# One store per tile, wv in row halves, and a new order of steps in an attention and channel-mix kernel

## Chip, cores and metric

The kernel runs on one core of one Trainium2 chip. The metric is the device time of one execution in microseconds (us), as the median over several runs.

## What is computed

An attention with 32 memory slots per head feeds a channel-mix block. Eight batches, eight heads, 576 tokens of 64 values per head; the heads side by side make 512 columns, and the channel mix widens these to 1024.

```python
# q, k, v: (8, 8, 576, 64), phi: (8, 8, 576, 32)
a = softmax(phi, axis=tokens)
k_m = einsum('bhsm,bhsd->bhmd', a, k);  v_m = einsum('bhsm,bhsd->bhmd', a, v)
attn = softmax(q @ k_m.T / sqrt(64), axis=slots)
x = heads_side_by_side(attn @ v_m)               # (8, 576, 512)
x_prev = x shifted by one token (zero at the first)
xk = mu_k * x + (1 - mu_k) * x_prev              # the same for xr with mu_r
k = relu(xk @ w_k)                               # w_k: 512 x 1024
out = sigmoid(xr @ w_r) * (k * k @ w_v)          # w_r: 512 x 512, w_v: 1024 x 512
```

## The kernel before

All arithmetic on the matrix engine is in bf16; the loads from HBM convert from f32 on the way and are issued by GpSimd (`nc.gpsimd.dma_start`), since they cast. The first batch's phi is loaded from ScalarE's queue, and the two short vectors mu_k and mu_r, as four rows of 128 values each, from SyncE's queue (L147, L148).

The order of the work is written out by hand. `PLAN` is a list of words, and each word emits the instructions of one step; every engine works through its own instructions in the order in which they were emitted. The words are of these kinds:

- `p:k:1`, `p:wk:4-8` and the like issue a load: k, v, q or phi of a batch, or columns of a weight (in blocks of 128). `preload` is their function.
- `0:...` to `7:...` are steps of the attention of one batch: `exp` (exponential of phi on ScalarE), `k`, `v`, `ko`, `kov` (sums over the tokens, tile kvps, L279), `z`, `zk` (reciprocals), `nk`, `ak` (normalised k by VectorE or by ScalarE), `tk`, `ta` (its transposition), `q0`, `q1` (transposition of q on VectorE), `s`, `s0`, `s1` (scores and their exponential), `f..`, `q..` and `y..` (the sum over the slots, its reciprocal and the weighting, on VectorE), and for batch 0 `mk`, `mr` (the mixing with the previous token, tile mxps, L245) and `busy21x4` (21 idle matmuls of 4 blocks of 128 columns, L215, which fill time in which the matrix engine has nothing else).
- `x1:...` to `x8:...` build chunks of 512 tokens of x (`v`), the difference to the previous token (`d`) and the mixed inputs for keys and gates (`k`, `r`).
- `c0:5a`, `c1:3` and the like are keys: one block of 128 of the 1024 columns for one chunk of tokens (L617), the relu on ScalarE (L621) and the square on VectorE, or on ScalarE where the word ends in `s`.
- `g:5` is the gate of a tile of 128 tokens (L650, L653).
- `o:5` is the value and output of a tile: eight matmuls over the 1024 rows of wv (L667), one step on VectorE that multiplies by the gate into an f32 tile `o` (L669), and the store (L602). `o:1a` and `o:1b` are the left and the right half of the columns of tiles 0 to 3; the last tile, 35, is done in two halves too.

There are 36 tiles of 128 tokens. Tokens are held in an order in which a block of 64 neighbouring places stands for every ninth row of a batch, so a tile of 128 places is two blocks of 64 rows in HBM, and `store` issues one transfer for each block, from SyncE's queue; for the last two tiles the second block goes through ScalarE's queue. Four buffers hold `o`, four hold the gate `sg`, and `BANKS` gives the PSUM bank of every step that needs one. The squares `sq` are a ring of nine tiles, the mixed inputs a ring of four batches.

Of the kernel before, what the change touches and what calls it, by code (L numbers as in the profile page):

```python
# [10 lines left out]
F32 = mybir.dt.float32  # L11
# [5 lines left out]


PLAN = [
# [24 lines left out]
]  # L44

LOADS = {None: ("phi", "k", "v", "q")}
PRE = "k:0a id:"
BANKS = (
    "01234567012367540123675403612754036127546203715462073154620731546207315462037416520374165724031567240315"
    "67203415672034162053472053416720534720516372401637254016354106732541067325410673254173254173065412730652"  # L50
    "73041652730416527304165274163052741630527416305276413052764130527641305276413"
)


NJ = 9
# [6 lines left out]
def kernel(  # L62
# [13 lines left out]
    nc = tc.nc  # L76
    B, H, S, D = q.shape
    M = phi.shape[-1]
    Dm = H * D
    Dff = moe_w_k.shape[1]  # L80
    NTOK = B * S
    scale = 1.0 / (D ** 0.5)
    ND = Dm // 128
    NF = Dff // 128
    NPAIR = H // 2
    QR = S // NJ
# [10 lines left out]
    psum = ctx.enter_context(tc.psum_pool(name="psum", bufs=1))  # L97
# [4 lines left out]
    def bank():  # L102
        return f"ps{next(banks)}"
# [16 lines left out]
    def load_phi(b, eng):  # L120
        ph = ld.tile([128, HH, NJ, M], F32, name="ph", tag=f"ph{b % 2}")
        eng.dma_start(out=ph.rearrange("p h j m -> p h (j m)"), in_=rows(phi[b]))
        loads[b] = ph

    def load_rows(dst, src):
        nc.gpsimd.dma_start(out=dst.rearrange("p h j d -> p h (j d)"), in_=rows(src))
# [25 lines left out]
    wv_sb = big.tile([128, NF, Dm], BF16, name="wv")  # L152
# [7 lines left out]
    def preload(word):  # L160

        what, _, part = word.partition(":")
        if what in weights:
            dst, src = weights[what]
            f0, f1 = (int(x) * 128 for x in part.split("-"))
            nc.gpsimd.dma_start(out=dst[:, :, f0:f1], in_=src[:, :, f0:f1])
        elif what == "id":
            make_identity(nc, identity)
        else:
            n = int(part[0])  # L170
            if what == "phi":
                load_phi(n, nc.gpsimd)
            else:
                dst = qs[n % 2].rearrange("p (h j) d -> p h j d", j=NJ) if what == "q" else kvs[:, KV[n % 2]["k1v".index(what)]]
                src = {"q": q, "k": k, "v": v}[what][n]
                if len(part) == 1:
                    load_rows(dst, src)
                elif part[1] in "ab":
                    load_parity(dst, src, ROWS["ab".index(part[1])])
                else:  # L180
                    gs = slice(2 * int(part[1]), 2 * int(part[1]) + 2)
                    nc.gpsimd.dma_start(out=dst[:, gs].rearrange("p h j d -> p h (j d)"), in_=rows(src)[:, gs])
# [16 lines left out]
    for g in range(4):  # L199
        r = slice(g * M, (g + 1) * M)  # L200
# [8 lines left out]
    sq = big.tile([128, NF, 2 * S], BF16, name="sq")  # L209
# [379 lines left out]
        return steps  # L589


    def store(o, t, cols):
        g = t * 128
        eng = nc.sync
        while g < (t + 1) * 128:
            b, r = divmod(g, S)
            p = g - t * 128
            j, p0 = divmod(r, QR)
            j = (j + 1) % NJ if b else j
            n = min(QR - p0, (t + 1) * 128 - g)  # L600
            dst = out[b].rearrange("(p j) d -> p j d", j=NJ)[p0:p0 + n, j, cols]
            eng.dma_start(out=dst, in_=o[p:p + n, cols])  # L602
            if t >= NTOK // 128 - 2:
                eng = nc.scalar
            g += n

    def keys(c):
        start = STARTS[c]
# [28 lines left out]
    gated, outs, homes, parts = {}, {}, {}, {}  # L637
    free = {"sg": list(range(SG)), "o": list(range(4))}

    def take(name, t):  # L640
        homes[name, t] = free[name].pop(0)
        return work.tile([128, Dm], F32, name=name, tag=f"{name}{homes[name, t]}")
# [10 lines left out]
            nc.scalar.activation(gated[t], pr, AF.Tanh, scale=0.5)  # L653
        return go

    def value(t, hs=((0, 1),), n=1):

        def go():
            if t not in outs:
                outs[t] = take("o", t)  # L660
            o = outs[t]
            p = t * 128 % (2 * S)
            for h0, h1 in hs:
                cols = slice(h0 * Dm // n, h1 * Dm // n)
                pv = psum.tile([128, Dm], F32, name="pv", tag=bank())
                for fi in range(NF):
                    nc.tensor.matmul(pv[:, cols], lhsT=sq[:, fi, p:p + 128],  # L667
                                     rhs=wv_sb[:, fi, cols], start=(fi == 0), stop=(fi == NF - 1))
                nc.vector.scalar_tensor_tensor(o[:, cols], in0=gated[t][:, cols], scalar=1.0, in1=pv[:, cols],  # L669
                                               op0=AL.add, op1=AL.mult)  # L670
                store(o, t, cols)
                parts[t] = parts.get(t, 0) + Dm * (h1 - h0) // n
            if parts[t] == Dm:
                for name in free:
                    free[name].append(homes[name, t])
        return go

    NT = NTOK // 128
    chunks = {f"x{c}": chunk_steps(c) for c in range(1, len(STARTS))}
    mixes = {f"c{c}": keys(c) for c in range(len(STARTS))}  # L680
    mixes["g"] = {str(t): gate(t) for t in range(NT)}
    mixes["o"] = {str(t): value(t) if t < NT - 1 else value(t, ((0, 1), (1, 2)), 2) for t in range(NT)}
    for t in range(4):
        for h in range(2):
            mixes["o"][f"{t}{'ab'[h]}"] = value(t, ((h, h + 1),), 2)

    attend = [attention(b) for b in range(B)]
    todo = []
    for n, word in enumerate(" ".join(PLAN).split()):
        who, _, name = word.partition(":")  # L690
# [40 lines left out]
```

## Time and profile before

| | |
|---|---|
| median of 3 runs | 201.68 us (201.15 to 201.99) |
| profiled execution, its own time | 200.59 us |
| its span from first to last instruction | 198.8 us |
| mean granted TensorE clock | 0.991 |
| TensorE busy | 189.0 us (95%) |
| VectorE busy | 155.5 us (78%) |
| ScalarE busy | 149.7 us (75%) |
| GpSimd busy | 29.8 us (15%) |
| DMA issues of the output | 79 from SyncE, 3 from ScalarE |
| HBM read, written | 38.28 MB, 9.44 MB |

How to read the lines below. PE is TensorE's matmuls, PEld its weight loads, DVE is VectorE, ACT is ScalarE, POOL is GpSimd and SP is SyncE; an engine's name with a q behind it is its queue of instructions. In the rows of digits the span is cut into 40 equal slices, and each digit is the busy share of a slice in tenths. A DMA queue's line gives packets, megabytes, and the time that its packets took as a share of 16 DMA engines' span; the DMA share of a stage is over 1 where packets overlap on an engine. In groups of instructions "x80 | 9.2, 273 | 0.0" is the count, the busy time in us, the mean of one in ns, and the idle time just before them. In lines in order of time the first two numbers are the start and the length in us, and brackets hold the idle time before it and what ended it. A line on DMA issues gives the count, the size on the SBUF side and the median us from issue to landing.

### The profile page before, as it was taken

The page shows a single profiled execution, that of the slowest core. Times are in us where ns is not written, and L with a number is a line of the kernel's source. Part 1 is how long each engine was busy: PE and PEld are TensorE (multiplying, and loading weights), DVE is VectorE, ACT ScalarE, POOL GpSimd, SP SyncE. Part 2 cuts the span into 40 slices and gives each one's busy share as a digit, 9 for nine tenths or more (in the row PEclk, how much of TensorE's full clock was granted, in tenths as well). Part 3 has the DMA queues.
Part 4 walks back from the last instruction along what each step waited for, and adds up shares of the span by engine and source line. Part 5 has one row for each costly group of instructions (what it writes and reads, how often), then busy time and mean ns, then how long its engine had stood idle before and what let it go on. Part 6 is the DMA issues. An engine that isn't in the chain of part 4 may idle for free.

```text
span 198.8 us, 5486 instructions
## 1 busy us (share of the span) xinstructions
PE 189.0 (95%) x2194; PEld 97.4 (49%) x2214; DVE 155.5 (78%) x428; ACT 149.7 (75%) x307; POOL 29.8 (15%) x45
## 2 busy tenths in 40 slices
PE   8978799999999999999999999999999999999992
PEld 3535565784454544445347644444443445444451
DVE  6179589898879998999699999998999998122232
ACT  2245899748987999999998899997878698935210
POOL 7843323211050210003500000000000000000000
PEclk9979999999999999999999999999999999999999
DMA  6999999999999999994999903212142027004345
GB/s 160 183 206 268 206 208 199 267 224 276 250 224 279 232 302 218 266 299 64 207 208 248 227 2 83 53 31 53 44 108 63 1 47 167 0 3 106 81 97 139
DMA packets 24522, 31.30 MB, mean 157 GB/s; under 512 B 1960, under 2 KB 19632, under 8 KB 24496
## 3 DMA queue, kind: packets, MB, share of 16 engines
q0 software_dynamic: 17392, 20.91, 56.4%
q1 hardware_dynamic: 6336, 9.18, 17.9%
q10 hardware_dynamic: 768, 0.85, 1.4%
q8 instruction: 17, 0.28, 0.5%
q14 instruction: 9, 0.07, 0.1%
HBM read 38.28 MB, written 9.44 MB: 240 GB/s over the span
## 4 chain that ended last, share of the span: by engine, by line
PE 70%; DMA 13%; DVE 9%; ACT 3%; issue 1%; POOL 1%; POOLq 0%; DVEq 0%
PE pv L667 26%; PE pk L617 25%; PE pr L650 13%; DMA wr<-in_moe_w_r_dram 9%; DMA q<-in_q_dram 4%; PE kvps L279 3%; DVE o L669 1%; DVE diff L545 1%; DVE sq L629 1%; PE scps L371 1%; PE nops L245 1%; ACT x L536 1%; ACT sg L653 1%; DVE xrT L567 1%; DVE lz L422 1%
## 5 line engine op out<-in xcount | busy, mean ns | idle before, releaser
L617 PE MATMUL pk<-xkT,wk 128*128 128x512 bf16 (+4 forms) x344 | 67.3, 340 | 1.0 <-ACT xkT L458 0.3
L667 PE MATMUL pv<-wv,sq 128*128 128x512 bf16 (+1 forms) x324 | 65.3, 353 | 0.2
L621 ACT ACTIVATE rl<-pk 128x512 bf16<-128x512 f32 (+3 forms) x80 | 42.9, 555 | 6.8 <-PE pk L617 4.2
L617 PEld LDWEIGHTS <-wk 128*128 128x128 bf16 x352 | 32.9, 98 | 29.3 <-issue 1.5
L667 PEld LDWEIGHTS <-sq 128*128 128x128 bf16 x328 | 31.4, 98 | 29.5 <-issue 0.4
L650 PE MATMUL pr<-wr,xrT 128*128 128x512 bf16 x136 | 34.8, 380 | 0.6 <-DMA wr<-in_moe_w_r_dram 0.2
L669 DVE SCALAR_TENSOR_TENSOR o<-sg,pv 128x512 f32<-128x512 f32 (+1 forms) x41 | 24.4, 614 | 11.5 <-PE pv L667 11.4
L560 ACT ACTIVATE mu_d<-diff,mu 128x512 bf16<-128x512 bf16 (+1 forms) x40 | 26.2, 716 | 6.1 <-DVE diff L550 2.9
L653 ACT ACTIVATE sg<-pr 128x512 f32<-128x512 f32 x36 | 20.9, 601 | 9.4 <-PE pr L650 5.7
L629 DVE TENSOR_TENSOR sq<-rl 128x320 bf16<-128x320 bf16 (+5 forms) x63 | 17.6, 314 | 12.2 <-ACT rl L621 11.9
L627 ACT ACTIVATE sq<-rl 128x512 bf16<-128x512 bf16 (+5 forms) x41 | 21.7, 543 | 1.1
L650 PEld LDWEIGHTS <-xrT 128*128 128x128 bf16 x144 | 13.5, 98 | 16.5 <-issue 0.8
L536 ACT CAST x<-nops 128x512 bf16<-128x512 f32 (+3 forms) x34 | 16.0, 572 | 2.0 <-PE nops L245 2.0
L431 DVE TENSOR_TENSOR atn<-e,lz 128x320 bf16<-128x320 bf16 (+1 forms) x32 | 13.2, 442 | 0.2
L545 DVE TENSOR_TENSOR diff<-x 128x1024 bf16<-128x1024 bf16 (+1 forms) x15 | 10.5, 699 | 2.6 <-ACT x L536 2.6
L422 DVE STREAM_TRANSPOSE lz<-se 128x320 f32<-128x320 f32 (+3 forms) x22 | 12.3, 572 | 0.2
L376 ACT ACTIVATE e<-scps 128x288 bf16<-128x288 f32 x32 | 10.5, 421 | 2.4 <-PE scps L371 2.4
L265 ACT ACTIVATE em<-ph 128x1152 bf16<-128x1152 f32 (+1 forms) x9 | 9.3, 1053 | 3.5 <-DMA ph<-in_phi_dram 3.5
L356 DVE STREAM_TRANSPOSE qT<-q 128x576 uint32<-128x576 uint32 x16 | 11.9, 757 | 0.0
L215 PE MATMUL idle<-zeros 128*128 128x512 bf16 (+2 forms) x44 | 10.9, 414 | 1.0 <-DVE zeros L144 1.0
L413 DVE TENSOR_REDUCE se<-eT 128x18 f32<-128x576 bf16 (+3 forms) x16 | 11.1, 696 | 0.2
L279 PE MATMUL kvps<-kvs,em 64*32 64x64 bf16 (+2 forms) x864 | 10.0, 220 | 1.2 <-DMA kvs<-in_k_dram 1.2
(72 smaller groups left out, 148.1 us busy)
## 6 DMA issues: line engine op xcount, KB each, us to landing
out_dram<-o SPq DMA_DIRECT2D x61, 128.0 KB, 2.5
kvs<-in_v_dram POOLq DMA_DIRECT2D x8, 576.0 KB, 15.5
ph<-in_phi_dram POOLq DMA_DIRECT2D x7, 576.0 KB, 18.8
kvs<-in_k_dram POOLq DMA_DIRECT2D x7, 576.0 KB, 19.0
q<-in_q_dram POOLq DMA_DIRECT2D x6, 576.0 KB, 18.9
q<-in_q_dram POOLq DMA_DIRECT2D x4, 288.0 KB, 10.1
out_dram<-o SPq DMA_DIRECT2D x18, 64.0 KB, 5.6
wk<-in_moe_w_k_dram POOLq DMA_DIRECT2D x2, 512.0 KB, 14.3
```

Source lines behind the costliest of these rows:

```text
L279: nc.tensor.matmul(kvps[c][g * M:(g + 1) * M], lhsT=em[ROWS[c], j, g, :], rhs=kvs[ROWS[c], at, g, j, :], start=j == 0, stop=j == NJ - 1, s ...
L422: nc.vector.transpose(st["lz"].rearrange("p c (b t h) -> p (c b) h t", t=PB, h=2)[:, b0:b0 + n], st["se"][:, b0:b0 + n].unsqueeze(3).to_br ...
L536: (nc.vector.tensor_copy if both and i % 2 else nc.scalar.copy)(x[:, i, c0:c1], pss[i])
L560: nc.scalar.activation(t[:, i, :n], ds[c][:, pr + i, :n], AF.Copy, scale=mu1[:, o:o + 1])
L617: nc.tensor.matmul(pk[:, p0 - lo:p1 - lo], lhsT=wk_sb[:, di, fi * 128:(fi + 1) * 128], rhs=xk_T[:, di, p0 % RING:p0 % RING + p1 - p0], sta ...
L621: nc.scalar.activation(rl, pk, AF.Relu, scale=HALF_ROOT)
L627: nc.scalar.activation(sq[:, fi, p:p + p1 - p0], rl[:, part], AF.Square)
L629: nc.vector.tensor_mul(sq[:, fi, p:p + p1 - p0], rl[:, part], rl[:, part])
L650: nc.tensor.matmul(pr, lhsT=xr_T[:, di, c0:c0 + 128], rhs=wr_sb[:, di, :], start=(di == 0), stop=(di == ND - 1))
L653: nc.scalar.activation(gated[t], pr, AF.Tanh, scale=0.5)
L667: nc.tensor.matmul(pv[:, cols], lhsT=sq[:, fi, p:p + 128], rhs=wv_sb[:, fi, cols], start=(fi == 0), stop=(fi == NF - 1))
L669: nc.vector.scalar_tensor_tensor(o[:, cols], in0=gated[t][:, cols], scalar=1.0, in1=pv[:, cols], op0=AL.add, op1=AL.mult)
```

## The change

- The second half of wv's columns (2-4) is loaded in two transfers, rows of the lower and of the upper half of its eight row blocks (`wv:2-4l`, `wv:2-4u`). The first half of the columns is loaded as before.
- For tiles 0 to 3 the value of half the columns can be worked out in two steps, over row blocks 0 to 3 and 4 to 7 of wv, which add into the same PSUM bank (`o:3e` then `o:3f`, `o:3c` then `o:3d`). The new order uses that for four of the eight halves, and takes tiles 0 to 3 otherwise in half columns as before. `value` also gains halves for the last four tiles; the new order uses `34a` and `34b`, and does tile 35 whole.
- `store` issues one transfer for a tile where its second block goes to higher rows than its first, with an access pattern of two blocks, 64 rows and the columns; where it does not (tiles 8, 17, 26 and 35), two transfers, both from SyncE's queue.
- `PLAN` and `BANKS` are written anew: the loads of batch 1's phi and k now come ahead of wk, the first half of wv ahead of v of batch 1, more idle matmuls stand in batch 0, and the steps of all batches, chunks, keys, gates and outputs stand in another order, with other choices between VectorE and ScalarE.

```diff
 PLAN = [
-    "0:exp0 p:k:0b 0:busy3x3 0:busy21x4 0:mu 0:mub 0:exp1 0:k0c 0:k1c p:q:00 0:z 0:ha0 0:busy2x2 p:q:01 0:hn1 0:q0",
-    "0:q1 0:hc1 p:v:0 0:ht0 0:s1 0:fe1 0:fs1 0:s0 0:busy8x2 0:fo1 0:l1 0:l0 0:y2 0:v 0:nr0 0:h1z 0:busy4x2 p:wk:4-8",
-    "0:nr1 p:phi:1 0:h0z 0:y0 0:busy6x2 0:nk0 0:nk1 0:y1 0:y3 0:mk0 p:q:11 p:k:1 0:mk1 c0:5a 1:exp c0:4a c0:6as",
-    "c0:7bs 0:mr1 1:ko 1:zk0 1:zk1 p:wk:0-4 1:nk p:q:10 c0:4b 1:q1 c0:7a 1:ta 0:mr0 c0:0a 1:q0 c0:0b c0:3b c0:1a",
-    "c0:2a 1:s1 p:wr:0-4 p:v:1 1:s0 1:fe1 1:fs1 c0:2b c0:3as 1:qo2 1:qe1 g:2 1:qs1 g:0 p:wv:0-2 1:qo3 1:y2 g:3 1:qe0",
-    "g:1 1:qs0 1:qo0 1:y0 c0:1b 1:qo1 1:y3 1:y1 1:v 1:av c0:5bs c0:6b x1:v0m o:1a x1:v1 x1:d2d o:3a x1:d0d p:wv:2-4",
...
-    "c8:1 c8:0s x8:r2d c8:5s c7:3s c7:5 g:35 c7:2s g:30 c7:0s c7:7 g:29 o:29 o:30 g:28 g:32 c8:7 c8:6s o:28 g:31 o:32",
-    "g:33 o:33 g:34 o:31 o:34 o:35",
+    "p:q:00 0:exp1 p:k:0b 0:exp0 0:busy30x4 0:z 0:k1c p:q:01 0:k0c 0:ha1 0:hc1 0:q0 0:q1 0:hn0 0:mub 0:s1 0:qe2 0:hc0",
+    "0:qe3 0:busy3x3 0:fs1 0:busy6x2 0:fo1 0:s0 p:v:0 0:busy4x1 0:y2 0:busy2x1 0:v1c 0:l0 0:l1 0:nr1 p:phi:1 p:k:1",
+    "0:v0c 0:h0z 0:y3 0:h1z 0:y0 0:nr0 0:y1 0:busy9x3 0:nk0 1:exp 0:nk1 0:mr0 0:mr1 1:ko0c 0:mk1 1:ko1c p:wk:4-8",
+    "1:zk1 0:mk0 p:wk:0-4 1:zk0 0:mu 1:nk c0:4bs c0:5a c0:5b c0:6a p:q:10 1:ta 1:q0 c0:4as c0:7bs c0:3b c0:0a c0:2b",
+    "p:q:11 c0:2as 1:q1 c0:1a c0:6b c0:1b 1:s1 1:qe2 1:qe3 p:wr:0-4 1:fs1 1:s0 1:qe1 1:qo3 c0:7as c0:0bs p:wv:0-2",
+    "1:qs1 c0:3as 1:qe0 1:qo2 1:qs0 g:1 1:qo0 1:qo1 g:3 1:y2 1:y1 g:2 1:y0 p:v:1 g:0 o:3e 1:y3 o:2a o:0a 1:v 1:nv",
+    "o:3f x1:v1m p:wv:2-4l o:3c x1:v0m p:wv:2-4u x1:d2d o:1e p:phi:2 x1:d0d x1:k0d x1:k2e 2:exp o:0c o:0d o:2b o:1f",
...
+    "x8:k0e o:25 c7:7s g:29 c7:1 x8:r0d x8:r2e c7:2 c8:6 c7:4s c7:3 c7:0 c8:3 c8:2s c8:5 g:28 c8:0 c8:7s g:33 c8:4s",
+    "g:31 c8:1s o:31 g:30 o:33 g:34 o:29 g:35 o:30 o:34b g:32 o:35 o:32 o:28 o:34a",
 ]
...
-            nc.gpsimd.dma_start(out=dst[:, :, f0:f1], in_=src[:, :, f0:f1])
+            fis = {"l": slice(0, NF // 2), "u": slice(NF // 2, NF)}.get(part[-1], slice(0, None))
+            nc.gpsimd.dma_start(out=dst[:, fis, f0:f1], in_=src[:, fis, f0:f1])
...
     def store(o, t, cols):
-        g = t * 128
-        eng = nc.sync
-        while g < (t + 1) * 128:
+        at = []
+        for g in (t * 128, t * 128 + QR):
             b, r = divmod(g, S)
-            p = g - t * 128
-            j, p0 = divmod(r, QR)
-            j = (j + 1) % NJ if b else j
-            n = min(QR - p0, (t + 1) * 128 - g)
-            dst = out[b].rearrange("(p j) d -> p j d", j=NJ)[p0:p0 + n, j, cols]
-            eng.dma_start(out=dst, in_=o[p:p + n, cols])
-            if t >= NTOK // 128 - 2:
-                eng = nc.scalar
-            g += n
+            at.append(b * S + ((r // QR + 1) % NJ if b else r // QR))
+        if at[0] < at[1]:
+            dst = flat[at[0]:, cols]
+            ap = [[(at[1] - at[0]) * Dm, 2], [NJ * Dm, QR], [1, cols.stop - cols.start]]
+            nc.sync.dma_start(out=bass.AP(tensor=dst.tensor, offset=dst.offset, ap=ap), in_=o[:, cols])
+        else:
+            for n, row in enumerate(at):
+                nc.sync.dma_start(out=flat[row:row + (QR - 1) * NJ + 1:NJ, cols], in_=o[n * QR:(n + 1) * QR, cols])
...
-    def value(t, hs=((0, 1),), n=1):
+    def value(t, hs=((0, 1),), n=1, f0=0, f1=NF):
...
+                pv = opened.get(t) if f1 - f0 < NF else None
+                fresh = pv is None
+                if fresh:
+                    pv = psum.tile([128, Dm], F32, name="pv", tag=bank())
...
+                for fi in range(f0, f1):
+                    nc.tensor.matmul(pv[:, cols], lhsT=sq[:, fi, p:p + 128], rhs=wv_sb[:, fi, cols],
+                                     start=(fi == 0 and fresh), stop=(fi == NF - 1),
+                                     skip_group_check=f1 - f0 < NF)
+                if f1 < NF:
+                    continue
```

More of the change, by code (lines that the diff above doesn't have):

```diff
@@ L48 @@
 BANKS = (
-    "01234567012367540123675403612754036127546203715462073154620731546207315462037416520374165724031567240315"
-    "67203415672034162053472053416720534720516372401637254016354106732541067325410673254173254173065412730652"
-    "73041652730416527304165274163052741630527416305276413052764130527641305276413"
+    "01234567012436571026453106274531026753106753104267531042675310426753104275310427531027463150274631502746"
+    "31502746315072314560314572603145726031426013426013426570134260134265703126570431265704365704123675012436"
+    "0124753601247536012475360124753601245736015234756021437560214375602143756021"
 )
@@ L164, in preload @@
             dst, src = weights[what]
-            f0, f1 = (int(x) * 128 for x in part.split("-"))
-            nc.gpsimd.dma_start(out=dst[:, :, f0:f1], in_=src[:, :, f0:f1])
+            f0, f1 = (int(x) * 128 for x in part.rstrip("lu").split("-"))
+            fis = {"l": slice(0, NF // 2), "u": slice(NF // 2, NF)}.get(part[-1], slice(0, None))
+            nc.gpsimd.dma_start(out=dst[:, fis, f0:f1], in_=src[:, fis, f0:f1])
         elif what == "id":
@@ L589, in chunk_steps @@
         return steps
+    flat = out.rearrange("b s d -> (b s) d")
     def store(o, t, cols):
-        g = t * 128
-        eng = nc.sync
-        while g < (t + 1) * 128:
+        at = []
+        for g in (t * 128, t * 128 + QR):
             b, r = divmod(g, S)
-            p = g - t * 128
-            j, p0 = divmod(r, QR)
-            j = (j + 1) % NJ if b else j
-            n = min(QR - p0, (t + 1) * 128 - g)
-            dst = out[b].rearrange("(p j) d -> p j d", j=NJ)[p0:p0 + n, j, cols]
-            eng.dma_start(out=dst, in_=o[p:p + n, cols])
-            if t >= NTOK // 128 - 2:
-                eng = nc.scalar
-            g += n
+            at.append(b * S + ((r // QR + 1) % NJ if b else r // QR))
[6 more added lines that the diff above has]
+                nc.sync.dma_start(out=flat[row:row + (QR - 1) * NJ + 1:NJ, cols], in_=o[n * QR:(n + 1) * QR, cols])
     def keys(c):
@@ L654, in gate @@
         return go
-    def value(t, hs=((0, 1),), n=1):
+    opened = {}
+    def value(t, hs=((0, 1),), n=1, f0=0, f1=NF):
         def go():
-            if t not in outs:
-                outs[t] = take("o", t)
-            o = outs[t]
             p = t * 128 % (2 * S)
@@ L664, in go @@
                 cols = slice(h0 * Dm // n, h1 * Dm // n)
[L665 to L668, printed above, removed]
+                pv = opened.get(t) if f1 - f0 < NF else None
+                fresh = pv is None
+                if fresh:
+                    pv = psum.tile([128, Dm], F32, name="pv", tag=bank())
+                if f1 - f0 < NF:
+                    opened[t] = pv
+                for fi in range(f0, f1):
[4 more added lines that the diff above has]
+                    continue
+                if t not in outs:
+                    outs[t] = take("o", t)
+                o = outs[t]
                 nc.vector.scalar_tensor_tensor(o[:, cols], in0=gated[t][:, cols], scalar=1.0, in1=pv[:, cols],
@@ L672, in go @@
                 parts[t] = parts.get(t, 0) + Dm * (h1 - h0) // n
-            if parts[t] == Dm:
+            if parts.get(t) == Dm:
                 for name in free:
@@ L681 @@
     mixes["g"] = {str(t): gate(t) for t in range(NT)}
-    mixes["o"] = {str(t): value(t) if t < NT - 1 else value(t, ((0, 1), (1, 2)), 2) for t in range(NT)}
+    mixes["o"] = {str(t): value(t) for t in range(NT)}
+    for t in range(NT - 4, NT):
+        for name, h, n in (("a", (0, 1), 2), ("b", (1, 2), 2), ("i", (0, 3), 4), ("j", (3, 4), 4)):
+            mixes["o"][f"{t}{name}"] = value(t, (h,), n)
     for t in range(4):
@@ L685 @@
             mixes["o"][f"{t}{'ab'[h]}"] = value(t, ((h, h + 1),), 2)
+            mixes["o"][f"{t}{'ec'[h]}"] = value(t, ((h, h + 1),), 2, 0, NF // 2)
+            mixes["o"][f"{t}{'fd'[h]}"] = value(t, ((h, h + 1),), 2, NF // 2, NF)
+        mixes["o"][f"{t}l"] = value(t, f1=NF // 2)
+        mixes["o"][f"{t}u"] = value(t, f0=NF // 2)
     attend = [attention(b) for b in range(B)]
```

32 rows, old and new, of the table PLAN are left out of this document.

## The prediction

> **What bounds the kernel now.** I read the page first, then busy time by stage, then the DMA answers of short windows.
>
> ```profile
> PE 189.0 (95%) x2194; PEld 97.4 (49%) x2214; DVE 155.5 (78%) x428; ACT 149.7 (75%) x307; POOL 29.8 (15%) x45
> PE   8978799999999999999999999999999999999992
> DMA  6999999999999999994999903212142027004345
> q0 software_dynamic: 17392, 20.91, 56.4%
> q1 hardware_dynamic: 6336, 9.18, 17.9%
> ```
>
> TensorE is the bound: 189.0 of 198.8 us. The 9.8 us that it idles lie at the two ends of the second row. The third row shows a second limit behind it: the 16 DMA engines are full from the first slice to about 115 us and have room only after that. So there is little to gain on TensorE, and much to lose if a transfer is made slower.
>
> ```profile
> 10.00:15.00 5.00, 3.85 (x51) 1.89 (x48) 3.58 (x9) 2.05 (x6) 2.13 (x3) 0.73 1.22 207
> 15.00:20.00 5.00, 4.27 (x129) 2.78 (x129) 4.66 (x13) 2.73 (x9) 1.83 (x3) 0.93 1.17 267
> 20.00:25.00 5.00, 3.84 (x118) 2.71 (x123) 2.61 (x11) 4.29 (x11) 1.50 (x2) 1.00 1.23 207
> 25.00:30.00 5.00, 4.59 (x85) 2.97 (x80) 4.29 (x13) 4.55 (x14) 1.48 (x2) 1.00 1.23 207
> ...
> 5.00:38.00 33.00, 29.49 (x600) 18.09 (x600) 23.64 (x66) 22.35 (x58) 13.21 (x18) 0.95 1.24 219
> 38.00:97.00 59.00, 58.43 (x857) 30.09 (x863) 53.69 (x140) 51.44 (x106) 12.46 (x17) 1.00 1.09 237
> 97.00:115.00 18.00, 17.89 (x203) 11.00 (x198) 16.96 (x53) 16.33 (x31) 0.20 (x1) 1.00 1.11 217
> 115.00:198.80 83.80, 79.18 (x537) 36.67 (x542) 58.17 (x158) 58.10 (x114) 0.00 (x0) 1.00 0.28 64
> ```
>
> After the span follow TensorE's busy time, then the other engines', the granted clock, the DMA share and GB/s. TensorE idles 0.73 + 1.16 + 0.41 = 2.3 us between 15 and 30 us, 0.57 us from 38 to 97 and 0.11 us from 97 to 115; of the last stage's 4.6 us, 3.8 are the tail after the last matmul. The DMA share is 1.24, 1.09, 1.11, then 0.28.
>
> **The stores.** Before, a tile of 128 tokens leaves in two stores of 64 rows. After, where the two blocks go to rising rows, one store carries both, and its pattern on the HBM side begins with a dimension of size 2 (two blocks), then 64 rows. What sets how many engines a store runs on?
>
> ```profile
> DMA packets 173, 0.19 MB, mean 66 GB/s; under 512 B 4, under 2 KB 173, under 8 KB 173
> q1 hardware_dynamic: 8, 0.00, 0.3%
> mu<-in_moe_mu_k_dram SPq DMA_DIRECT2D x1, 2.0 KB
> ```
>
> ```profile
> DMA packets 160, 0.26 MB, mean 66 GB/s; under 512 B 32, under 2 KB 32, under 8 KB 160
> q1 hardware_dynamic: 160, 0.26, 28.8%
> ```
>
> ```profile
> GB/s 197 262 246 164 164 49 0 0 0 164 279 131 197 197 197 377 434 303 344 254 164 221 271 279 230 148 8 0 0 0 0 0 0 0 0 0 0 0 0 0
> ```
>
> These are the DMA answers for 0 to 2.9 us, 184 to 188 us and 194 to 199 us. In the first window SyncE's queue (q1) moved 8 packets, and 4 packets of all were under 512 bytes: the mu load of four rows of 512 bytes is four row packets and four small completion packets. In the second, one tile's two stores are 128 row packets and 32 small ones: 16 completions for each store of 64 rows. The page's 6336 is the same count: 79 × (64 + 16) + 2 × (4 + 4). So the engines on which a transfer runs follow the size of its outermost dimension: 4 for four rows, 16 for sixty-four. I read from this that an outermost size of 2 gives two engines. No run here shows a pattern of 2 on one side with 128 on the other, so this is an inference, and the main one. The Trainium skill ("DMA: Bandwidth & Descriptors", section "Why a DMA increments its semaphore by 16 and not by 1") says it outright: the engine count is the largest number up to 16 that divides the slowest dimension of both sides. By that rule it is two; the trace agrees for 4 and 16.
>
> Price on two engines. Of 36 tiles, four (8, 17, 26, 35) have falling rows and keep two stores; 32 are merged. The 9.18 + 0.26 MB of all stores are 0.262 MB a tile, so 8.39 MB are merged, 4.19 MB for each of two engines instead of 0.52. The best slice of the third fence moved 434 GB/s, 27.1 an engine: 4.19 MB take 155 us, 4.8 us a tile. From the other side, the second window's 28.8% of 4 us on 16 engines for 128 rows is 144 ns a row, and 64 rows one after another are 9.2 us a tile, 295 us in all. I take 155: that 144 ns is with 16 engines writing at once. The skill's page gives 27 GiB/s for an engine; by that figure it would be an estimated 145 us.
>
> The same two engines carry a sixteenth each of every load. 20.91 MB at the 219 GB/s of 5 to 38 us are 95.5 us, the same on each engine. The four unmerged tiles add 2.4 us (1.05 MB on 16 engines at 27.1). Sum on either engine: 95.5 + 155 + 2.4 = 253 us, more than the whole span now. A load has landed only when its slowest engine is done, so from the first store (about 38 us) on every load runs at the pace of those two. I allow 1.7 us ahead of the first load's packets (an estimate within the first window's 2.9), and the third fence's last packets lie 1.4 us before the end: 1.7 + 253 + 1.4 = 256 us of span. The profiled execution lasted 200.6 us for a span of 198.8, and lies 1.1 us under the median of 201.7: 256 + 1.8 + 1.1 = 259 us.
>
> What waits then: a store that has not landed holds one of four o buffers; the vector step at L669 (`scalar_tensor_tensor` into o) waits for the buffer, and behind it on VectorE stand the attention, squares and mixing of the next chunk, on which TensorE's keys wait.
>
> **What removing stores saves.** 79 + 3 issues become about 46, at about 0.63 us of queue time each (1.89 for three, below). SyncE's queue does nothing else, so that is worth nothing except at the end.
>
> ```profile
> 194.03 1.89 SPq L602 DMA_DIRECT2D out_dram<-o  x3
> 194.04 2.04 ACTq L602 DMA_DIRECT2D out_dram<-o  x3
> 195.01 0.42 DVE L669 SCALAR_TENSOR_TENSOR o<-sg,pv 128x256 f32<-128x256 f32 x1 [0.45 <-PE pv L667]
> ```
>
> Now the last half tile (35) leaves by two queues at once; after, half of tile 34 leaves in one store from SyncE, 0.66 us behind tile 28's (0.92 of matmul, 9.2 us for ten half tiles in the next fence, + 0.42 − 0.68 of vector time). On 16 engines I book 0 (−0.3 to +0.6); on two engines it is in the sum above.
>
> **wv in row halves and values in two steps.**
>
> ```profile
> L667 PE MATMUL pv<-wv,sq 128*128 128x256 bf16 x80 | 9.2, 273 | 0.0
> L669 DVE SCALAR_TENSOR_TENSOR o<-sg,pv 128x512 f32<-128x512 f32 x31 | 20.5, 678 | 10.9 <-PE pv L667 10.9
> ...
> L166 POOL DMA_DIRECT2D wv<-in_moe_w_v_dram x2: 873/878/884, 17.1 to 18.6; - x2
> L215 PE MATMUL idle<-zeros 128*128 128x512 bf16 x21 | 6.5, 479 | 0.0
> L215 PE MATMUL idle<-zeros 128*128 128x256 bf16 x20 | 3.5, 331 | 0.0
> L215 PE MATMUL idle<-zeros 128*128 128x384 bf16 x3 | 1.1, 516 | 1.0 <-DVE zeros L144 1.0
> ```
>
> Splitting a value into fi 0–3 and 4–7 leaves its eight matmuls as they are, so TensorE pays nothing; one bank stays taken between the steps, covered while seven others turn. One load more is 0.88 us of GpSimd, which is 15% busy: hidden. The idle matmuls grow from 133 to 174 blocks of 128 columns; 11.1 us for 133 make 41 more cost 3.4 us. They stand where TensorE waits for the first loads, which hides them; uncovered, they cost up to 3.4.
>
> **Order at the front.**
>
> ```profile
> 6.01 0.80 POOL L122 DMA_DIRECT2D ph<-in_phi_dram  x1
> 6.76 0.75 POOL L182 DMA_DIRECT2D q<-in_q_dram  x1
> 7.45 0.82 POOL L126 DMA_DIRECT2D kvs<-in_k_dram  x1
> ```
>
> ```profile
> ph<-in_phi_dram POOLq DMA_DIRECT2D x1, 576.0 KB, 12.3
> q<-in_q_dram POOLq DMA_DIRECT2D x1, 288.0 KB, 12.8
> ```
>
> ```profile
> kvs<-in_k_dram POOLq DMA_DIRECT2D x1, 576.0 KB, 15.5
> ```
>
> ```profile
> 17.50 1.36 PE L245 MATMUL mxps<-atn,vm 32*64 32x320 bf16 x40 [0.36 <-DVE vm L441]
> 19.12 2.32 PE L617 MATMUL pk<-xkT,wk 128*128 128x320 bf16 x16 [0.26 <-ACT xkT L458]
> 21.37 0.42 PE L245 MATMUL mxps<-atn,vm 32*64 32x256 bf16 x16
> 22.96 0.80 PE L279 MATMUL kvps<-kvs,em 64*32 64x128 bf16 x72 [1.16 <-DMA kvs<-in_k_dram]
> 24.88 0.48 PE L245 MATMUL mxps<-atn,vm 32*64 32x320 bf16 x24
> 29.97 3.63 PE L650 MATMUL pr<-wr,xrT 128*128 128x512 bf16 x15 [0.22 <-DMA wr<-in_moe_w_r_dram]
> ```
>
> GpSimd's queue hands loads over in order. Before, half of wk comes ahead of batch 1's phi and k, and k lands at 7.45 + 15.5 = 22.95. After, phi and k come first and the q half (1.3 us: 19.6 against phi's 18.3) moves behind wk, so the first half of wk lands near 22.95 − 1.3 = 21.6, and the first key, now at 19.12, starts 2.5 us later. TensorE has for that gap the mixing of r (0.42 + 0.48 us) and batch 1's k sums (0.80), 1.7 us; and the 1.16 us wait goes, since k lands early. Net 2.5 − 1.7 − 1.16 = −0.4 us. Up to wr the bytes are the same, so wr stays at 29.9, and the keys, three of whose halves now run behind the gates (L650), fill the time up to it. Behind 38 us TensorE idles under 1 us until 115, so no order gains more than that. It can cost: VectorE is busy 53.69 of 59 us and 16.96 of 18 there, so a vector step put late delays keys by its own length, 0.4 to 0.7 us; I book 0 and leave it to the second rival.
>
> **Rivals.** *First, the merged stores run on 16 engines* (the generator splits by the 128 rows on the SBUF side, or cuts the transfer in two, so that the change does not do what it says in the hardware). For it: each 64-row block alone ran on 16; against it: the count of 4 above. Then only the front is left: −0.4 and, where the order closes all of the 2.3 us, −2.3; in the middle 201.7 − 1.35 = 200.3 us, faster. It decides whether mixing r is done when wk lands at 21.6.
>
> *Second, the same without the luck*: batch 0's scores are split, its second half standing behind the mu matmuls and a copy on ScalarE, so the mixing starts late and the extra idle matmuls delay it in place of covering it. If mixing of k begins after about 20.2 us (21.6 less its 1.36), TensorE loses up to the 3.4 us; with half of it 203.4 us, slower.
>
> *Third, two engines but overlapped*: a load packet and a store packet run on one engine at the same time. A DMA share of 1.24 hints at it, though packets also just last longer when many run. Then 253 / 1.24 = 204 of engine time, and about 210 us.
>
> **How the numbers follow.** Two engines with loads and stores in turn: 0.45, 259 us, its own range 225 to 285. Two engines overlapped: 0.07, 210. Sixteen engines: 0.48, of which faster by over 0.5% 0.22, within 0.5% 0.09, slower 0.17 by the second rival. 0.5%, 1.0 us, is about what a measurement of this kernel can tell from no change. So faster 0.22, same 0.09, slower 0.45 + 0.07 + 0.17 = 0.69. The range must hold both cases: 199 leaves out about 0.08 below, 285 about 0.08 above, where a row costs nearer 144 ns.
>
> **What would show it.** Two engines: SyncE's queue shows 130 packets for a merged store (128 rows and 2 completions) where a tile has 160 now; landing is over 5 us instead of 2.5; the load phase runs past 150 us; TensorE's row loses its 9s; and waits for `out_dram` stand high at L669. Sixteen engines: 144 packets a store, landing under 4 us, and the DMA row thin after 115 us as now. The front is right if wk lands near 21.6 and kvps no longer waits for k. I am wrong in the main thing if merged stores land like the old ones.

## The result: 281.56 us, and the profile after

The changed kernel takes **281.56 us** (median of four runs, 281.32 to 282.48) against 201.42 us for the kernel before (200.89 to 201.99): a ratio of **1.399 [1.393, 1.404]**. Its profiled execution lasted 281.62 us, with a span of 279.8 us and a mean granted clock of 0.865 (before: 200.59, 198.8, 0.991). L669 of before is L681 of after, L617 is L619, L650 is L652, L667 is L673.

The page of after, first the busy times and three of the rows of 40 slices (7.0 us each), then the queues, the chain and two lines of the DMA issues:

```profile
PE 208.4 (74%) x2224; PEld 103.7 (37%) x2224; DVE 157.6 (56%) x437; ACT 153.1 (55%) x319; POOL 30.4 (11%) x46
PE   8998999994058699419999871579999999993000
DMA  7999999939911953112499711121111121111211
GB/s 147 210 239 205 202 247 253 213 61 232 209 39 48 189 111 115 51 51 66 89 247 223 140 37 41 51 84 54 41 51 53 33 76 54 33 51 51 84 51 41
...
q0 software_dynamic: 17408, 20.91, 40.5%
q1 hardware_dynamic: 5466, 9.44, 10.1%
...
DMA out_dram<-o 42%; PE pk L619 17%; PE pv L673 9%; PE pr L652 7%; PE idle L217 5%; DVE o L681 2%; PE kvps L281 2%; PE scps L373 1%; ACT mu_d L562 1%; PE mxps L247 1%; DVE diff L547 1%; PE nops L247 1%; DVE qT L358 0%; DVE se L415 0%; PE ktps L340 0%
...
out_dram<-o SPq DMA_DIRECT2D x27, 256.0 KB
...
out_dram<-o SPq DMA_DIRECT2D x18, 128.0 KB
```

TensorE, the bound before, has holes of whole slices and is busy 74% of the span. The bytes of both queues are what they were (20.91 MB in, 9.44 MB in all out). Of the chain that ended last, 42% of the span, 117 us, is now stores of o: on the page of before no transfer has such a share.

How many engines carry a merged store can be counted. The 45 stores are 27 merged tiles, 10 merged half tiles and 8 stores of 64 rows (27 + 10 + 8; the 18 of 128 KB are the last two kinds). With 130 packets for a merged store, 128 rows and two completions, 37 × 130 + 8 × (64 + 16) + 2 × (4 + 4) = 5466, which is q1's number exactly. With sixteen engines it would be 37 × 144 in place of 37 × 130, and 5984 in all.

Their speed stands in the GB/s row: a level of 51, with the DMA digit at 1, since 2 of 16 engines is 0.125. The DMA answer for 200 to 260 us, where almost only stores run, gives the same: 1500 packets in 60 us, at 130 packets a tile one tile in 5.2 us.

```profile
q1 hardware_dynamic: 1500, 2.97, 14.9%
```

What that costs is seen in three stages of after, in the columns of the prediction's table of stages (length, busy time of PE, PEld, DVE, ACT, POOL, granted clock, DMA share, GB/s):

```profile
38.00:97.00 59.00, 40.62 (x626) 21.43 (x624) 34.05 (x93) 32.98 (x69) 6.88 (x10) 0.87 0.78 159
...
150.00:200.00 50.00, 35.88 (x389) 16.65 (x387) 31.03 (x93) 27.81 (x59) 0.00 (x0) 0.83 0.33 77
...
260.00:279.80 19.80, 0.00 (x0) 0.00 (x0) 1.02 (x2) 0.00 (x0) 0.00 (x0) 0.50 0.18 59
```

From 38 to 97 us TensorE works 40.62 us where it worked 58.43 before, and issues 626 matmuls where it issued 857. At the end lie 19.8 us in which it does nothing; before, that tail was 3.8. The waits of after (us in total, times, longest) name what stands between:

```profile
DVE o L681 <- DMA out_dram<-o: 63.9, 14, 17.5
POOL kvs L127 <- PE kvps L281: 47.3, 3, 24.8
POOL kvs L127 <- PE nops L247: 31.7, 1, 31.7
...
PE pv L673 <- DVE o L681: 14.6, 1, 14.6
```

VectorE stands 63.9 us at the step into o because all four o buffers are in stores that have not landed. TensorE runs dry behind it. GpSimd then stands with the next loads (second and third line), because their buffers are freed by TensorE: so the loads, which could have run beside the slow stores, do not start. The chain of waits shows the stretches (start, length):

```profile
51.46 28.11 DMA out_dram<-o
82.06 10.98 DMA out_dram<-o
...
99.05 25.50 DMA out_dram<-o
...
152.82 29.27 DMA out_dram<-o
...
239.31 23.27 DMA out_dram<-o x2
```

The pieces from 51 to 93, 99 to 125, 153 to 182 and 239 to 263 us are the 42%. The chain ends there; the last stores land up to 278.6 us.

### The profile page after: what moved, and what is told of

Read it like the earlier page. It is cut to its first block, busy times and chain, and to the rows that moved or that the text cites. A ratio compares the mean times of both kernels' runs of the same rounds, so it can differ in the third digit from the quotient of the medians.

```text
span 279.8 us, 5510 instructions
## 1 busy us (share of the span) xinstructions
PE 208.4 (74%) x2224; PEld 103.7 (37%) x2224; DVE 157.6 (56%) x437; ACT 153.1 (55%) x319; POOL 30.4 (11%) x46
## 3 DMA queue, kind: packets, MB, share of 16 engines
q0 software_dynamic: 17408, 20.91, 40.5%
q1 hardware_dynamic: 5466, 9.44, 10.1%
HBM read 38.28 MB, written 9.44 MB: 171 GB/s over the span
## 4 chain that ended last, share of the span: by engine, by line
PE 43%; DMA 42%; DVE 7%; ACT 1%; issue 1%; DVEq 0%
DMA out_dram<-o 42%; PE pk L619 17%; PE pv L673 9%; PE pr L652 7%; PE idle L217 5%; DVE o L681 2%; PE kvps L281 2%; PE scps L373 1%; ACT mu_d L562 1%; PE mxps L247 1%; DVE diff L547 1%; PE nops L247 1%; DVE qT L358 0%; DVE se L415 0%; PE ktps L340 0%
## 5 line engine op out<-in xcount | busy, mean ns | idle before, releaser
L619 PE MATMUL pk<-xkT,wk 128*128 128x512 bf16 (+4 forms) x352 | 76.2, 370 | 13.4 <-DVE o L681 9.7
L673 PE MATMUL pv<-wv,sq 128*128 128x512 bf16 (+1 forms) x328 | 68.0, 361 | 15.8 <-DVE o L681 14.6
L681 DVE SCALAR_TENSOR_TENSOR o<-sg,pv 128x512 f32<-128x512 f32 (+1 forms) x41 | 24.9, 618 | 75.6 <-DMA out_dram<-o 63.9
L623 ACT ACTIVATE rl<-pk 128x512 bf16<-128x512 f32 (+3 forms) x80 | 42.0, 553 | 22.2 <-PE pk L619 21.6
L619 PEld LDWEIGHTS <-wk 128*128 128x128 bf16 x352 | 35.5, 105 | 46.6 <-issue 22.8
L673 PEld LDWEIGHTS <-sq 128*128 128x128 bf16 x328 | 31.9, 99 | 47.8 <-issue 17.8
L562 ACT ACTIVATE mu_d<-diff,mu 128x512 bf16<-128x512 bf16 (+1 forms) x44 | 28.6, 721 | 27.4 <-DVE diff L552 17.7
L652 PE MATMUL pr<-wr,xrT 128*128 128x512 bf16 x144 | 36.2, 387 | 0.0
L631 DVE TENSOR_TENSOR sq<-rl 128x512 bf16<-128x512 bf16 (+5 forms) x58 | 17.6, 332 | 10.0 <-ACT rl L623 9.7
L652 PEld LDWEIGHTS <-xrT 128*128 128x128 bf16 x144 | 14.0, 100 | 17.0 <-issue 2.2
L281 PE MATMUL kvps<-kvs,em 64*32 64x64 bf16 (+2 forms) x864 | 11.7, 222 | 4.9 <-DMA kvs<-in_k_dram 3.4
L217 PE MATMUL idle<-zeros 128*128 128x512 bf16 (+3 forms) x54 | 13.7, 420 | 1.0 <-DVE zeros L145 1.0
L424 DVE STREAM_TRANSPOSE lz<-se 128x256 f32<-128x256 f32 (+2 forms) x27 | 12.8, 491 | 0.2
L281 PEld LDWEIGHTS <-em 64*32 64x32 bf16 x864 | 9.2, 91 | 9.0 <-issue 7.8
L373 PE MATMUL scps<-qT,kmT 32*32 32x288 bf16 x256 | 5.9, 316 | 7.9 <-DVE o L681 5.4
L127 POOL DMA_DIRECT2D kvs<-in_v_dram x8 | 6.0, 754 | 50.5 <-PE kvps L281 47.3
## 6 DMA issues: line engine op xcount, KB each, us to landing
q<-in_q_dram POOLq DMA_DIRECT2D x6, 576.0 KB, 19.1
```

The costliest lines, as they stand in the source:

```text
L217: nc.tensor.matmul(ps.rearrange("p (a b) -> p a b", b=128), lhsT=zeros, rhs=zeros.unsqueeze(1).to_broadcast([128, blocks, 128]), start=Tru ...
L281: nc.tensor.matmul(kvps[c][g * M:(g + 1) * M], lhsT=em[ROWS[c], j, g, :], rhs=kvs[ROWS[c], at, g, j, :], start=j == 0, stop=j == NJ - 1, s ...
L562: nc.scalar.activation(t[:, i, :n], ds[c][:, pr + i, :n], AF.Copy, scale=mu1[:, o:o + 1])
L619: nc.tensor.matmul(pk[:, p0 - lo:p1 - lo], lhsT=wk_sb[:, di, fi * 128:(fi + 1) * 128], rhs=xk_T[:, di, p0 % RING:p0 % RING + p1 - p0], sta ...
L623: nc.scalar.activation(rl, pk, AF.Relu, scale=HALF_ROOT)
L631: nc.vector.tensor_mul(sq[:, fi, p:p + p1 - p0], rl[:, part], rl[:, part])
```

## The experiments

All are compared with the kernel before on the same chip, which took 200.5 to 200.8 us. The letters of the theories in the expectations: A, the outermost size sets the number of engines; B, a pattern of two levels is slow whatever its sizes; C, the new order of steps is the cause; D, the time of loads and stores on the two engines, summed, sets the end; E, stores are squeezed while loads are queued, the o buffers fill, VectorE stands and the loads then run out; F, the idle matmuls are in the way at the front; G, they keep the clock up; H, wk comes late.

**Stores or order?** The first takes the merged store out of after and keeps the rest; the second puts it into before and changes nothing else but the queue of the last two tiles' second stores, which is SyncE's as in after.

```diff
-        if at[0] < at[1]:
+        if False:            # two stores of 64 rows for every tile
```

> The changed kernel with two stores of 64 rows for every tile, both from SyncE: the rest of the change by itself. Theory A (a merged store runs on two engines): all but a few us of the 80 go; 201 to 207 us, since the front of the changed trace reaches its first gate at 36.1 us instead of 30.0 with three more key halves (1.3 us) done, and nothing of that has to do with stores. Theory C (the new order is the cause): 260 us or more. The DMA answer of a lone tile shows 160 packets.

> The kernel before with nothing but the merged store, from SyncE. Theory A: 270 to 290 us, as in the changed kernel, since 32 tiles of 5.1 us on two engines (256 KB at the 51 GB/s of the changed kernel's late stage) are 164 us wherever the steps stand. Theory C: 201 to 203 us.

Measured: 204.33 us, ratio 1.016 [1.011, 1.021], and 274.55 us, 1.368 [1.361, 1.376]. The store alone, in the old order, brings 74 of the 80 us. C falls as the main cause. The rest of the change is not free either: it costs 1.6%, some 3 us (below).

**Two levels or the size 2?** Here every tile leaves in one store of two levels, with 16, 8 or 4 as the outermost size, from the same queue and with the same bytes. Only the pattern on the HBM side is another: a tile's rows go to neighbouring places, in all three alike, and no tile leaves in two stores.

```diff
-        if at[0] < at[1]:
-            dst = flat[at[0]:, cols]
-            ap = [[(at[1] - at[0]) * Dm, 2], [NJ * Dm, QR], [1, cols.stop - cols.start]]
+        if True:
+            dst = flat[t * 128:, cols]
+            ap = [[Dm, 16], [16 * Dm, 128 // 16], [1, cols.stop - cols.start]]
```

> The changed kernel, but each tile leaves in one store whose pattern on the HBM side begins with a dimension of 16, then 8 rows; a tile's rows go to other places among its 128 neighbouring rows, so the output is permuted. Theory A (engines follow the outermost size): 16 engines, 144 packets a store, about 0.7 us of transfer a tile, within 1% of the run with two stores. Theory B (a store with two levels of rows is slow whatever the sizes): 260 us or more.

> As the run with an outermost size of 16, with 4 and then 32 rows; rows permuted within a tile in the same way. Theory A: four engines, 132 packets a store, 102 GB/s in a late stretch, 2.6 us a tile, 92 us of stores on each of four engines beside some 95 us of loads: 188 us, under the span, so between 203 and 225 us. Theory B: 260 us or more.

> As the runs with an outermost size of 16 and of 4, with 8 and then 16 rows; rows permuted within a tile in the same way. By the engine count: eight engines, 136 packets a store, about 204 GB/s in a late stretch, 1.3 us a tile. With outermost sizes of 2, 4 and 16 the times were 281.6, 232.9 and 203.6 us; stores that get a small share while loads run, as with 4, would still hold the o buffers at times: 205 to 212 us.

Measured: 203.6 us with 16 (1.013 [1.008, 1.019]), 207.44 with 8 (1.033 [1.029, 1.037]), 232.92 with 4 (1.161 [1.154, 1.168]), after 281.56 with 2. B falls: a store of two levels and 16 outermost costs nothing. A stands, and the sizes order the times. The packets of q1 say it directly: each of the three has 41 stores (31 tiles and 10 half tiles), and 41 × (128 + 4) + 16, with 8 and with 16 in place of the 4, are its numbers:

```profile
q1 hardware_dynamic: 5428, 9.44, 12.2%
```

```profile
q1 hardware_dynamic: 5592, 9.44, 15.5%
```

```profile
q1 hardware_dynamic: 5920, 9.44, 16.1%
```

The Trainium skill's rule that the prediction cited ("DMA: Bandwidth & Descriptors", section "Why a DMA increments its semaphore by 16 and not by 1") holds in all four: the engine count is the largest divisor common to both sides' slowest dimensions, up to 16. The GB/s of the kernel with 4, from 170 to 200 us in 40 slices, have a level of about 102, twice the 51:

```profile
GB/s 57 96 82 71 71 123 96 57 11 0 0 0 0 0 0 0 0 0 0 11 33 11 38 74 101 101 104 101 104 104 98 106 101 98 106 112 27 0 0 0
```

But 232.9 misses the 203 to 225 that I had expected of 4 from the sum of engine times, 95.5 + 92.5 (9.44 MB at 102 GB/s) = 188 us, less than the span. So the sum alone does not make the time. The DMA answers for 48 to 56 us, where loads and stores are both queued, say why. The first two lines are after's q0 and q1, the next two are q1 with 4 and 8 outermost; the last is after's q1 from 84 to 91 us, where no load runs:

```profile
q0 software_dynamic: 1403, 1.57, 114.7%
q1 hardware_dynamic: 116, 0.12, 5.2%
```

```profile
q1 hardware_dynamic: 235, 0.23, 10.5%
```

```profile
q1 hardware_dynamic: 449, 0.43, 19.7%
```

```profile
q1 hardware_dynamic: 336, 0.34, 13.6%
```

In 8 us each engine that carries stores passes 58 of their packets in after (116 / 2), 59 with 4 (235 / 4) and 56 with 8 (449 / 8). They are rows of 1 KB of half tiles, so that is some 7 GB/s an engine. Without loads the same rows make 48 GB/s on two engines, 24 an engine. Beside queued loads a store on few engines takes some three times as long, and the buffers can fill though the sum has room.

How an engine divides its time is seen from 160 to 172 us of after, where about two engines are at work (DMA digit 1):

```profile
DMA  1111111111111121111111111111111113111111
...
q0 software_dynamic: 137, 0.15, 7.4%
q1 hardware_dynamic: 137, 0.28, 6.7%
```

There are as many load packets as store packets: the engines take one of each in turn. The stores, with rows of 2 KB, get 11.7 GB/s an engine, where they have 25.5 alone. And the last loads wait there for the two engines, though the others have nothing left to do.

In the waits of the kernel with 4, the step into o stands 24.7 us:

```profile
DVE o L681 <- DMA out_dram<-o: 24.7, 7, 6.4
```

With 8 no step waits for a store; why it takes 3 us more than with 16 stays open.

**Sum or buffers?** Six o buffers in place of four. To make room the zeros of the idle matmuls shrink to 32 columns.

```diff
-    free = {"sg": list(range(SG)), "o": list(range(4))}
+    free = {"sg": list(range(SG)), "o": list(range(6))}
```

> The changed kernel with six o buffers instead of four (and idle matmuls with 32 instead of 128 stationary columns, to make room). Theory D (the work of the two engines, loads and stores in turn, sets the end): 279 to 283 us, unchanged. Theory E (while loads are queued the stores get a small share of the two engines, the o buffers fill, VectorE stands, and then the loads have run ahead and wait in their turn, so that engine time is lost): two tiles more of slack in each stretch, 255 to 272 us.

Measured: 273.32 us, ratio 1.360 [1.350, 1.369], 8 us less than after, between the two expectations. VectorE's wait for stores fell from 63.9 to 33.7 us:

```profile
DVE o L681 <- DMA out_dram<-o: 33.7, 7, 9.4
```

Thirty microseconds of waits gone buy eight of time. So the two engines' own time is the larger part (D), and what the full buffers add the smaller (E). The eight are only in part accounted for. Between the first and the last store packet after has 2.7 us in which no packet of loads or stores is under way, this kernel has none. Its first gate starts at 34.26 us, after's at 35.94: that part lies at the front, whose idle matmuls this edit changes too.

**Only the late stores merged.** From tile 18 on, when most loads are through.

```diff
-        if at[0] < at[1]:
+        if at[0] < at[1] and t >= 18:
```

> The changed kernel with merged stores only for tiles 18 to 34, after the loads; tiles 0 to 17 leave in two stores. 16 merged tiles at 5.1 us are 82 us on two engines, in a stretch that lasts about 90 us now, but its last 12 tiles come every 3 us or less: both theories 215 to 230 us, nearly all of the loss at the end, with the vector step waiting for the store.

Measured: 225.32 us, 1.121 [1.113, 1.129]. Sixteen merged tiles behind the loads cost 21 us over none; the early ones cost the other 56. Off the loads' path the store is still no use: the chain ends in a train of stores, and from 185 us to the end the page's GB/s row is at 36 to 51 but for one slice of 91.

```profile
GB/s 157 189 260 206 206 203 255 248 245 234 172 246 234 300 210 296 44 9 187 309 232 199 62 89 46 28 53 54 51 29 82 54 38 41 51 51 91 50 51 36
```

**The same from GpSimd's queue**, as `nc.gpsimd.dma_start` for those late merged stores:

> As the run with merged stores for tiles 18 to 34, but those stores are issued by GpSimd, which has no load left to issue by then. If a merged store runs on two engines but each on another pair (what the Trainium skill's DMA page says of GpSimd's queue), several run side by side: 203 to 208 us. If it is the same pair again, or the two-level pattern itself is slow: 222 to 228 us as from SyncE.

Measured: 220.02 us, 1.097 [1.093, 1.102], outside both expectations. The DMA answer for 160 to 215 us, in which eleven of these 17 stores are issued:

```profile
GB/s 0 0 6 44 70 131 68 73 87 91 51 66 78 24 0 0 0 14 15 34 69 77 88 84 100 82 87 98 176 88 45 24 18 49 98 81 87 42 42 30
DMA packets 5594, 3.19 MB, mean 58 GB/s; under 512 B 4702, under 2 KB 4702, under 8 KB 5592
...
out_dram<-o POOLq DMA_DIRECT2D x9, 256.0 KB, 10.1
```

The stores run mostly at 66 to 100 GB/s, faster than the 51 of SyncE's, far from 16 engines. Most of the packets are under 512 bytes, and a store takes 10.1 us to land. So this queue cuts the transfer up in another way. On how many engines it lands is not visible in the trace and stays open.

**The 3 us that are not the store.** With two stores everywhere the rest of the change stood alone at 204.33. Three edits of that kernel look for its cost: no idle matmuls behind the first groups, no split of wv and of the first values, and the first half of wk ahead of batch 1's phi and k with the keys right behind.

```diff
-  0:busy3x3 ... 0:busy6x2 ... 0:busy4x1 ... 0:busy2x1 ... 0:busy9x3
+  0:busy0x3 ... 0:busy0x2 ... 0:busy0x1 ... 0:busy0x1 ... 0:busy0x3
```

> The run with two stores per tile, without the idle matmuls behind the first thirty (3x3, 6x2, 4x1, 2x1, 9x3). Theory F (idle matmuls stand in the way of batch 0's second scores and of the mixing, which start about 1.5 us late each at the clock then granted): 1 to 3 us faster than the run with two stores, 201 to 203 us. Theory G (they keep the clock up): the same or slower, keys at half clock after 20 us, 204 to 207 us.

```diff
-  o:3e ... o:3f ... p:wv:2-4l o:3c ... p:wv:2-4u ... o:1e ... o:0c o:0d ... o:1f o:3d
+  o:3a ... p:wv:2-4 ... o:0b ... o:1a o:3b
```

> The run with two stores per tile, with wv's second half of columns in one load and the values of tiles 0 to 3 in one step each. If the row halves and two steps do what they are for, 0.5 to 1 us slower (205 us); by the prediction's zero, the same within 0.5 us.

```diff
-  p:v:0 0:busy4x1 ... 0:nk0 1:exp 0:nk1 0:mr0 0:mr1 ... p:wk:4-8
+  p:v:0 p:wk:4-8 0:busy4x1 ... 0:nk0 0:nk1 0:mk1 0:mk0 c0:4bs c0:5a c0:5b c0:6a 1:exp 0:mr0 0:mr1
```

> The run with two stores per tile, with the first half of wk loaded ahead of batch 1's phi and k again, and the mixing of k and four key halves ahead of the mixing of r and batch 1's k sums, as in the kernel before. Theory H (the front lost its 3 us because wk lands at 21.6 instead of 16.8 and the keys start late, at a clock that has dropped): the first gate starts near 31 us instead of 34.3, 201 to 202.5 us. If the loss lies elsewhere in the new order: 204 to 205 us.

Measured: 204.86 us (1.019 [1.014, 1.023]), 205.76 (1.021 [1.016, 1.026]) and 205.69 (1.025 [1.021, 1.029]). None gains anything. The one without the split is 1.4 us above the 204.33, with overlapping intervals: what row halves and two steps are worth is not settled.

Where the 3 us lie is clear, why they do is only half clear. The first gate matmul starts at 34.33 us with two stores everywhere, where it started at 29.97 before:

```profile
34.33 2.97 PE L652 MATMUL pr<-wr,xrT 128*128 128x512 bf16 x12
```

Ahead of it stand 12 more key matmuls of 256 columns, 1.3 us at the 0.108 us each that eight of 512 in 1.73 us make. That leaves 3.1 us lost before 35 us. Two things are seen there. One is the clock. The first two rows are the kernel with two stores, the last two the one without the later idle matmuls:

```profile
15.00:20.00 5.00, 5.00 (x105) 2.79 (x104) 3.14 (x8) 1.95 (x6) 1.71 (x3) 0.50 1.20 209
20.00:25.00 5.00, 4.65 (x134) 2.66 (x134) 3.33 (x10) 2.84 (x8) 1.42 (x2) 0.74 1.23 207
```

```profile
15.00:20.00 5.00, 3.27 (x102) 1.78 (x90) 4.84 (x14) 4.01 (x11) 1.53 (x2) 0.50 1.21 210
20.00:25.00 5.00, 4.65 (x117) 3.24 (x118) 2.28 (x8) 1.66 (x5) 1.48 (x2) 0.50 1.23 207
```

Before, these stretches had 0.93 and 1.00. Without the idle matmuls the clock stays at 0.50 for both, and what their absence frees is lost again: F falls. G is not simply right either: with the idle matmuls the clock was 0.50 from 15 to 20 us too, though TensorE was busy for all 5.00. The other is the place of the keys: with 16 outermost the clock was 1.00 up to 20 us, and the first gate still came at 34.09. H in its plain form fell with the last of the three edits: in the execution of it that was profiled, of 207.95 us, the keys began at 21.66 and the first gate at 37.82, not near 31. So I leave it at this: late keys and a dropped clock, in shares that differ from one version to the next.

## Why the prediction was right, and where it was not

**Two engines: right, and shown.** The inference from four rows and sixty-four was carried on to a size that no trace had, and the count of 5466, the 51 GB/s and the series 16, 8, 4, 2 bear it out. The first rival, sixteen engines, fell. So did the third: overlap would have given 210.

**The price of a store: 6% low.** I took the best slice of before, 27.1 GB/s an engine; after's level is 51 GB/s on two, 25.5. The 8.39 MB take 164.5 us in place of 155. The other end, 9.2 us a tile, is refuted by the 5.2.

**"Every load runs at the pace of those two": borne out where a load ends.** In all, the loads hardly slow down: from 38 to 60 us they moved 4.20 MB, 191 GB/s, and with two stores of 64 rows 4.14 MB, since fourteen engines have no merged store to share with. But a load is there only when its last packet is, and from 160 to 172 us the last loads come in at one packet for each store packet on two engines. The longest landing of a load of q is 33.3 us, with two stores everywhere 21.1. The prediction's sum needs no order, since two engines that are always busy need the same time in any. What it leaves out is what the order does to the rest of the core: the o buffers fill, VectorE and TensorE stand, and the next loads wait for free buffers.

Put into the prediction's sum, 95.5 + 164.5 + 2.4 + 1.7 + 1.4 make a span of 265.5 us; it was 279.8. So the miss of 23.8 us in the span is 9.5 from the rate of the stores and 14.3 from elsewhere. Little of the 14.3 is idle time of the two engines. Counted by the packets of loads and stores in the trace, between the first store packet at 45.8 us and the last at 278.6 none is under way for 2.7 us and a single one for 2.0. The longest hole lies in the GB/s row for 216 to 224 us, in slices of 0.2 us:

```profile
GB/s 41 61 41 61 41 61 41 61 41 61 41 61 41 61 41 61 20 31 10 0 0 0 0 41 0 0 0 0 41 20 20 31 61 20 82 20 31 61 41 51
```

Other slices of the page's row that lie under 51 are no holes: those of 84 to 91 us are rows of 1 KB, and those of 160 to 172 us hold load packets in turn with the stores. Two us more go by at the start, where the first packet of GpSimd's loads comes at 3.7 us and not at 1.7: batch 0's phi from ScalarE's queue (0.59 MB) runs ahead of it, and the sum leaves that out. The rest, some 8 us, would be the loads' own time on the two engines, by the 13.7 GB/s an engine (219 / 16) being too high for the later ones. That is what is left over; no run separates it.

So the mechanism was right and the sum too small. The range held 281.6 us by 3.4, and its upper end had been set for rows that cost nearer 144 ns, which none did. That it covers the terms that were missing is luck.

**What waits: right.** The step into o (L669, now L681) waits for `out_dram`, 63.9 us, and the chain runs through it. The load phase runs past 150 us, as the slices of 247 and 223 GB/s from 140 to 154 us show.

**The front: times right, balance wrong.** Batch 1's k and the first half of wk were issued and landed so (the rows of GpSimd's queue in after, and the DMA answer for their issues):

```profile
6.07 0.78 POOL L127 DMA_DIRECT2D kvs<-in_k_dram  x1
6.81 0.79 POOL L168 DMA_DIRECT2D wk<-in_moe_w_k_dram  x1
```

```profile
kvs<-in_k_dram POOLq DMA_DIRECT2D x1, 576.0 KB, 13.0
wk<-in_moe_w_k_dram POOLq DMA_DIRECT2D x1, 512.0 KB, 14.8
```

That is 6.81 + 14.8 = 21.6 us for wk, as forecast; k is there at 19.1, and its wait is gone. But the net of −0.4 us became a loss: the step that filled the gap with the mixing of r and batch 1's k sums assumed full speed and no other gap. With two stores the mixing of r began at 22.46, behind idle matmuls from 19.47 to 22.5, and that of k at 24.18. That is the second rival's condition (after 20.2), and its price of 203.4 is close to the 204.33. In after the mixing of r began at 19.55 and that of k at 21.32, and the first keys, at 25.08, ran at half clock (0.50 from 25 to 29 us): 16 matmuls of 256 columns in 4.02 us, where before eight of the same took 1.15.

```profile
23.32 0.93 PE L281 MATMUL kvps<-kvs,em 64*32 64x128 bf16 x27 [1.31 <-issue]
...
25.08 4.02 PE L619 MATMUL pk<-xkT,wk 128*128 128x256 bf16 x16
```

The run without the later idle matmuls gained nothing, so the 3.4 us that the prediction set for them uncovered is not what the front lost; that its size is near is luck.

**The tail and the halved issues.** On 16 engines one store a tile is worth no more than two: 203.6 us against 204.33, with overlapping intervals. SyncE's queue had nothing else to do, as the prediction booked.

## What to carry to other kernels

Before two transfers are merged into one pattern, look at the size of the outermost dimension of the merged pattern: here 2 in place of 64 rows left a store two of sixteen engines, and the fewer instructions were worth nothing. Packets per transfer show it at once (rows plus one completion for each engine), and so does a DMA row that stays at 1 with a flat GB/s level. And a sum of engine times below the span doesn't make a slow store free: beside queued loads its packets take turns with theirs, so price it by how long it holds its buffer, and by who waits for that buffer.

## What the hardware showed that I had not expected

Stores and loads take turns on a shared engine, packet for packet: 137 and 137 from 160 to 172 us. So what a store gets depends on the size of its rows: some 7 GB/s an engine with rows of 1 KB and 11.7 with 2 KB beside queued loads, 24 and 25.5 alone.

A merged store from GpSimd's queue ran at 66 to 100 GB/s where SyncE's ran at 51, with thousands of packets under 512 bytes.

And in a front full of loads TensorE stood with nothing to wait for that the profile shows: the 1.31 us above, 1.20 us in the kernel without the split, and 1.95 us in the kernel with 16 outermost.

```profile
22.80 0.57 PE L281 MATMUL kvps<-kvs,em 64*32 64x128 bf16 x27 [1.95 <-issue]
```

Ahead of it one packet of instructions (q8) was under way among the loads. That TensorE waited for it is my reading; no run took it away.
